# Sorted-block attention with a SwiGLU layer on one core: one weight load cut in two, a smaller mixing matrix, and a new order for the first scores

## The chip, the core and the metric

The kernel runs on one core of a Trainium2 chip. A core has five engines that run side by side, each with its own list of instructions in order: TensorE (PE; its weight loads are shown apart as PEld), VectorE (DVE), ScalarE (ACT), GpSimd (POOL) and SyncE (SP). Sixteen DMA engines move data between DRAM and the core's memory. TensorE writes its results into PSUM, eight banks of 512 float32 values in each of 128 partitions. The metric is the time of one execution in microseconds (us) on the device; less is better.

## The reference

Inputs are q, k and v of shape (4, 8, 768, 64): 4 batches, 8 heads, 768 rows of 64; a matrix sort_net of 8 x 8 for each batch and head; and three weight matrices. Everything is float32.

```python
P = sort_net
for _ in range(5):                       # Sinkhorn: rows, then columns
    P = P - np.max(P, axis=-1, keepdims=True)
    P = np.exp(P)
    P = P / (np.sum(P, axis=-1, keepdims=True) + 1e-09)
    P = P / (np.sum(P, axis=-2, keepdims=True) + 1e-09)
k_sorted = np.einsum('bhij,bhjcd->bhicd', P, k_b)     # 8 blocks of 96 rows are mixed
v_sorted = np.einsum('bhij,bhjcd->bhicd', P, v_b)
scores = scale * np.matmul(q_b, k_sb.transpose(0, 1, 2, 4, 3))   # within each block
attn = softmax(scores)
x = concat_heads(np.matmul(attn, v_sb))               # 3072 tokens x 512
g = x @ w_gate                                        # 512 x 1536
val = x @ w_val
out = (g / (1 + exp(-g)) * val) @ w_out               # 1536 x 512
```

So there is a small normalisation of P, a mixing of key and value blocks by P, attention inside each block of 96 rows, and a SwiGLU layer (FFN) over all 3072 tokens.

## The kernel before, in words

**FFN.** The 3072 tokens are taken as eight token tiles of 384 (`ffn(n)`, n = 0 to 7). In a tile the 1536 hidden columns are taken 128 at a time, m = 0 to 11. `gate(n, m)` (matmuls on L410) and `value(n, m)` (L428) each make four matmuls. ACT takes the tanh (L418), DVE makes the product with the gate (L420) and the product with the value (L433). The output projection of a tile (`outp`, L445) runs during the next tile.

**Attention.** `scores(b, u)` (L332) makes the scores of a unit u of batch b, a unit being 4 blocks of two heads; `exps` takes the exponential on ACT, in one instruction where the two heads sit in one two-bank tile (L345) and in two otherwise (L343). `av` multiplies by the values (L359), and DVE divides by the row sums (reciprocal L363, product `st` L365). The result is transposed (`x_first`, `x_to`, L376) and becomes the FFN's input `xt`.

**Mixing.** Keys, values and queries are brought into the layout that attention wants by matmuls with a block-diagonal matrix `rmix`, in chunks: `q0_chunk` (L274), `k0_chunk` (L284), `v_chunk` (L300) for batch 0, `kq_chunk` (L264) for later batches. A chunk is drained from PSUM by DVE (L242) or ACT (L244), as its argument "v" or "s" says. `vch` holds the values in another layout; POOL (L150) and ACT (L148) copy it from the loaded `v`. `rmix` is made from the Sinkhorn result: DVE writes `p_bf`, the 8 x 8 matrices with eight copies side by side (L236); 16 matmuls (L494) turn this into `w_ps`, 64 rows at a time; `mix_rows` (L499) masks it.

**PSUM tiles** are named by a tag: "a" and "b" hold two banks each, "gen" has three buffers of one bank, "x" is one bank. A new tile in a tag waits until the readers of the one before it have finished.

**The start (L483 to L582)** is written out by hand for TensorE, DVE, ACT and POOL: the order in the source is the order on the engine. Matmuls on zeros (`fill`, and `wide_fill` in float32) stand in places where TensorE has nothing to do. Then `merge` puts attention and mixing of later batches between the FFN's matmuls at written-out times; from there on the planner orders DVE, and TensorE, POOL, ACT and SP keep the source's order.

**Loads.** Nearly all loads are issued by POOL into one queue, with a conversion from float32 to bfloat16 on the way. In order: v of batch 0 (1, 2), q (3), k in two halves (4, 5), then after POOL's three copies into `vch` the weights. `load_gv(lo, hi)` loads the columns lo to hi of the gate weights and then of the value weights (L136): 0 to 255 (loads 6, 7), q again (8), 256 to 511 (9, 10), 512 to 1023 (11, 12), 1024 to 1535 (13, 14), then the first half of v of batch 1 (15). After three mixes on POOL and 16 one-element memsets (`pad`, L509) come k, q and v of batch 1 (16 to 20), the output weights `wo` (21 to 23, L516), and four copies of v of batch 1 into `vch` (L150), which `v_chunk(1, ...)` in `ffn(1)` reads. `kq_chunk(1, ...)` reads k and q of batch 1. SP's queue has the first load of sort_net and later the output stores and transposes.

Of the kernel before, what the change touches and what calls it, by code (L numbers as in the profile page):

```python
# [9 lines left out]
FP32 = mybir.dt.float32  # L10
BF16 = mybir.dt.bfloat16
AF = mybir.ActivationFunctionType
ALU = mybir.AluOpType
# [4 lines left out]
def kernel(  # L18
# [11 lines left out]
    nc = tc.nc  # L30

    B, H, S, D = q.shape
    NB = sort_net.shape[-1]
    C = S // NB
    BH = B * H
# [18 lines left out]
    const = ctx.enter_context(tc.tile_pool(name="const", bufs=1))  # L54
# [83 lines left out]
    def load_gv(lo, hi):  # L138
        load_w(wg_sb, wg_dram, lo, hi)
        load_w(wv_sb, wv_dram, lo, hi)  # L140
# [38 lines left out]
    load_gv(0, 256)  # L179
    load_q0(1)  # L180
    load_gv(256, 512)
    load_gv(512, 1024)
    load_gv(1024, DF)
    load_v(1, 0, 2)

# [6 lines left out]
    def vt_tile(pair):  # L192
        if pair not in vts:
            t = vtp.tile([C, 2, H * NB, D + 8], BF16, name=f"vt{pair}", tag="vt")
            nc.vector.memset(t[:, :, :, D:D + 1].rearrange("p u n e -> p (u n) e"), 1.0)
            vts[pair] = t
        return vts[pair]
# [6 lines left out]

    rowreds = [const.tile([BH, NB, 1], FP32, name=f"rowred{it}") for it in range(N_ITER)]
    colred = const.tile([BH, 1, NB], FP32)
    p_bf = const.tile([BH, NB, 8, NB], BF16)
    w_sb = const.tile([128, NB, B, H], BF16)
    pad = const.tile([1, 16], FP32)
    def pair_tile(name, tag):  # L210
        return psum.tile([128, 1024], FP32, name=name, tag=tag)

# [3 lines left out]
    p_ps = bank_tile("p_ps")[0:BH, 0:NB * NB].rearrange("p (i j) -> p i j", j=NB)  # L216
    for it in range(N_ITER):
        nc.scalar.activation(p_ps, p_sb if it == 0 else p_ps, AF.Exp)
        if it == 1:
            with nc.allow_low_precision("0/1 mask"):  # L220
                nc.vector.tensor_reduce(mask, id4, axis=AX.XY, op=ALU.add)
            nc.scalar.copy(sel, ident.rearrange("p (r g two) -> p two g r", g=H2, two=2))
        if it == 2:
            copy_v(nc.scalar, 0, lowr, 0, cs=slice(24, 34))
            vt_tile(1)
        if it == 3:
            copy_v(nc.scalar, 0, lowr, 0, cs=slice(34, 46))
        rowred = rowreds[it]
        nc.vector.reduce_sum(rowred[:, :, 0], p_ps, axis=AX.X)
        nc.vector.reciprocal(rowred, rowred)  # L230
        nc.vector.tensor_mul(p_ps, p_ps, rowred.to_broadcast([BH, NB, NB]))
        nc.vector.reduce_sum(colred[:, 0, :], p_ps.transpose([0, 2, 1]), axis=AX.X)
        nc.vector.reciprocal(colred, colred)
        if it < N_ITER - 1:
            nc.vector.tensor_mul(p_ps, p_ps, colred.to_broadcast([BH, NB, NB]))
    nc.vector.tensor_tensor(p_bf, p_ps.unsqueeze(2).to_broadcast([BH, NB, 8, NB]),  # L236
                            colred.unsqueeze(1).to_broadcast([BH, NB, 8, NB]), op=ALU.mult)
    copy_v(nc.scalar, 0, lowr, 0, d1=40, cs=slice(46, 72))

    def drain(eng, dst, src):  # L240
# [28 lines left out]
    def q0_chunk(t, at, n, eng, tag):  # L269
        dst = kqt_tile(0)[:, GI * C:2 * GI * C].rearrange("p (g t r c) -> p t g r c", g=H2, t=2, c=QC)[:, t]  # L270
        tp = chunk_tile("tq0", n // 8, tag).rearrange("p (l g r) -> p l g r", l=n, g=H2)
        for lc in range(n):
            for two in range(2):
                nc.tensor.matmul(tp[two * D:(two + 1) * D, lc], lhsT=q0[t][:, at + lc, :],  # L274
                                 rhs=sel[:, two], start=True, stop=True)
        drain(eng, dst[:, :, :, at:at + n], tp.rearrange("p l g r -> p g r l"))

    def k0_chunk(at, n, eng, tag, parts=None):
        dst = kqt_tile(0)[:, 0:GI * C].rearrange("p (n a c) -> p a n c", a=2, c=HC)
        rm = rmix[0].rearrange("p a (g two) i -> p two a g i", two=2)  # L280
        tp = chunk_tile("tk0", n // 8, tag).rearrange("p (l a n) -> p l a n", l=n, a=2)
        for lc in range(n):
            for two in range(2):
                nc.tensor.matmul(tp[two * D:(two + 1) * D, lc].rearrange("p a (g i) -> p a g i", g=H2),  # L284
                                 lhsT=k0[:, at + lc, :], rhs=rm[:, two], start=True, stop=True)
        src = tp.rearrange("p l a n -> p a n l")
        if parts is None:
            drain(eng, dst[:, :, :, at:at + n], src)
            return
        drain(eng, dst[:, :, 0:parts, at:at + n], src[:, :, 0:parts])  # L290
        return lambda e: drain(e, dst[:, :, parts:, at:at + n], src[:, :, parts:])

    def v_chunk(b, at, n, eng, tag):
        rows = slice(0, 128) if b % 2 else lowr
        dst = vt_tile(b // 2)[:, b % 2]
        mix = rmix[b][rows, 0].rearrange("p a b -> p (a b)")
        tp = chunk_tile("tv", n // 8, tag).rearrange("p (l n) -> p l n", n=H * NB)
        for ld in range(n):
            col = (at + ld) * C
            nc.tensor.matmul(tp[:, ld, :], lhsT=vch[rows, col:col + 128], rhs=mix,  # L300
                             start=True, stop=True)
        drain(eng, dst[:, :, at:at + n], tp[0:C].transpose([0, 2, 1]))
# [45 lines left out]
    def qk(b, u, tag="b"):  # L348
        exps(b, u, *scores(b, u, tag))

    def av(b, u, tag="a"):
        half, g = divmod(u, H2)
        vt = vts[b // 2][:, b % 2].rearrange("p (h i) e -> p h i e", h=H)
        av_ps = pair_tile("av_ps", tag).rearrange("p (two n) -> p two n", two=2)
        o = av_ps.rearrange("p two (i e) -> p two i e", i=4)
        for two in range(2):
            e = es[(b, u)][two]
            for i4 in range(4):
                nc.tensor.matmul(o[:, two, i4, 0:D + 1], lhsT=e[:, i4 * C:i4 * C + 128],  # L359
                                 rhs=vt[:, 2 * g + two, half * 4 + i4, 0:D + 1],  # L360
                                 start=True, stop=True)
        r_sb = ssp.tile([C, 2, 4, 1], FP32, name="r_sb", tag="r")
        nc.vector.reciprocal(r_sb, o[0:C, :, :, D:D + 1])  # L363
        st = ssp.tile([C, 4, 2, D], BF16, name="st", tag="st")
        nc.vector.tensor_tensor(st.rearrange("p i two d -> p two i d"), o[0:C, :, :, 0:D],  # L365
                                r_sb.to_broadcast([C, 2, 4, D]), op=ALU.mult)
        sts[(b, u)] = st
# [105 lines left out]
    idle_ps = bank_tile("idle_ps", "x")  # L473

    def fill(tile, n):
        for _ in range(n):
            nc.tensor.matmul(tile, lhsT=warm_sb[:, 0:128], rhs=warm_sb, start=True, stop=True)

    def wide_fill(n):
        for _ in range(n):  # L480
            nc.tensor.matmul(idle_ps, lhsT=wide_sb[:, 0:128], rhs=wide_sb, start=True, stop=True)  # L481

    wide_fill(3)  # L483
    nc.tensor.matmul(idle_ps[0:8, 0:8], lhsT=vch[lowr, 24:32], rhs=vch[lowr, 24:32], start=True, stop=True)
    wide_fill(1)
    fill(idle_ps, 3)
    q0_chunk(0, 0, 8, "s", "x")
    fill(bank_tile("idle_ps"), 2)

    w_ps = bank_tile("w_ps")[:, 0:NB * B * H].rearrange("p (i b h) -> p i b h", b=B, h=H)  # L490

    for i in range(NB):
        for g in range(2):
            nc.tensor.matmul(w_ps[64 * g:64 * g + 64, i].rearrange("p b h -> p (b h)"),  # L494
                             lhsT=p_bf[:, i].rearrange("p a b -> p (a b)"),
                             rhs=ident[0:BH, 0:BH], start=True, stop=True)

# [7 lines left out]
    for b in range(1, B):  # L505
        rows = halves[b % 2]
        mix_rows(nc.gpsimd, rmix["p"][rows, b % 2] if b > 1 else rmix[1][rows, 0], rows, w_sb, b)
    for n in range(16):
        nc.gpsimd.memset(pad[:, n:n + 1], 0.0)  # L509
    for lo, hi in ((0, 2), (2, 4)):  # L510
        load_k(1, lo, hi)
# [12 lines left out]
    k0_chunk(8, 8, "v", "gen")  # L524
    k0_chunk(16, 8, "s", "gen")
    k0_chunk(24, 8, "v", "gen")
    rest = [k0_chunk(32, 8, "s", "x", 2 * NB), k0_chunk(40, 8, "v", "gen", 2 * NB)]
    v_chunk(0, 40, 16, "v", "b")
    v_chunk(0, 56, 8, "s", "gen")
    for drain_rest in rest:  # L530
        drain_rest("v")
    fill(pair_tile("idle_ps", "a")[:, 0:512], 1)
    qk(0, 0, "a")
    qk(0, 1, "b")
    av(0, 0, "a")
    qk(0, 2, "gen")
    idle_ps = bank_tile("idle_ps", "x")
    fill(idle_ps, 1)
    av(0, 1, "b")
    xts[(0, 0)] = xtp.tile([128, H2, TW], BF16, name="xt0_0", tag="xt")  # L540
    qk(0, 3, "mixed")

    def x_first(u, eng, tag):
        x_ps = xt_tile(tag, 1)[:, 0]
# [34 lines left out]
    value_out(0, 1, first[3])  # L579
    q0_chunk(1, 0, 16, "s", "b")  # L580
    q0_chunk(1, 16, 8, "v", "x")
    nc.vector.tensor_copy(rmix[1][lowr, 1].rearrange("p h i -> p (h i)"), ident[lowr, lowr])  # L582
    man.__exit__(None, None, None)
    man = tc.manual_schedule(engines={ET.PE, ET.Pool, ET.Activation, ET.SP})
# [112 lines left out]
```

## Time and profile before

| | |
|---|---|
| Time, median of 3 runs | 244.59 us (244.46 to 245.49) |
| The profiled execution | 243.93 us, its span 242.2 us |
| TensorE busy | 232.7 us (96%) |
| DVE, ACT, POOL busy | 155.6, 112.0, 54.9 us |
| First matmul of the FFN (L559) | at 21.05 us |
| First full gate by `gate` (L410) | at 25.16 us |
| Copies of v of batch 1 into `vch` on POOL | 37.90 to 49.16 us |

All times inside an execution are counted from the start of its span. In a line of the timeline the first number is the start in us, the second the length, then engine, source line, operation, what it writes and reads, their shape and how many instructions were joined; in brackets how long the engine was idle before, and what released it. "Landing" is the moment at which the data of a load is in place; the trace has it for every load.

### The profile page before, as it was taken

How to read it: one execution, taken by the hardware profiler on the slowest of the kernel's cores; microseconds unless marked ns; L12 is line 12 of the kernel's file. 1: busy time of each engine (PE TensorE's matmuls, PEld its weight loads, DVE VectorE, ACT ScalarE, POOL GpSimd, SP SyncE). 2: the span in 40 equal slices, each digit the busy share in tenths (PEclk: the TensorE clock that was granted, in tenths of full speed). 3: DMA queues.
4: the chain of work that ended last, by engine and by line, in shares of the span. 5: the costliest groups of instructions: out<-in, count | busy, mean ns of one | idle time of the engine just before them, and what ended most of it. 6: DMA issues, size and time to landing. Idle time of an engine off the chain costs nothing.

```text
span 242.2 us, 5881 instructions
## 1 busy us (share of the span) xinstructions
PE 232.7 (96%) x2453; PEld 136.8 (56%) x2476; DVE 155.6 (64%) x327; ACT 112.0 (46%) x190; POOL 54.9 (23%) x66
## 2 busy tenths in 40 slices
PE   7789999999999999999999999999999999999994
PEld 3376665775556556555555565565556555555543
DVE  6796889874666585776855765484566477445700
ACT  3977652577526434455454253345325433332212
POOL 5997228970006089000000000000000000000000
PEclk9999999999999999999999999999999999999999
DMA  5989999999936999462122112012111211110122
GB/s 96 214 120 181 206 213 211 206 211 202 174 92 132 186 164 152 90 129 71 37 72 63 35 43 77 3 60 64 35 41 55 67 37 43 43 43 3 43 87 87
DMA packets 40698, 24.76 MB, mean 102 GB/s; under 512 B 29408, under 2 KB 35424, under 8 KB 40672
## 3 DMA queue, kind: packets, MB, share of 16 engines
q0 software_dynamic: 20688, 14.16, 41.2%
q1 hardware_dynamic: 19840, 10.17, 16.7%
q8 instruction: 19, 0.31, 0.5%
q10 hardware_dynamic: 144, 0.07, 0.1%
q14 instruction: 7, 0.06, 0.1%
HBM read 28.32 MB, written 7.86 MB: 149 GB/s over the span
## 4 chain that ended last, share of the span: by engine, by line
PE 85%; DMA 7%; POOL 5%; issue 1%; DVE 1%; ACT 0%; POOLq 0%
PE v_ps L428 25%; PE g_ps L410 25%; PE o_ps L445 24%; DMA wv_sb<-in_moe_w_val_dram 5%; POOL vch L150 3%; PE tkq L264 3%; PE av_ps L359 3%; PE qk L332 2%; DMA v<-in_v_dram 2%; PE tv L310 1%; PE o_ps L461 1%; POOL wg_sb L136 1%; PE tv L300 1%; POOL wv_sb L136 1%; PE x_ps L376 0%
## 5 line engine op out<-in xcount | busy, mean ns | idle before, releaser
L420 DVE SCALAR_TENSOR_TENSOR gs_sb<-th_sb,g_ps 128x384 bf16<-128x384 bf16 x96 | 52.9, 551 | 50.1 <-ACT th_sb L418 47.1
L410 PE MATMUL g_ps<-xt,wg_sb 128*128 128x384 bf16 x376 | 76.6, 325 | 0.1
L428 PE MATMUL v_ps<-xt,wv_sb 128*128 128x384 bf16 x376 | 76.5, 326 | 0.1
L418 ACT ACTIVATE th_sb<-g_ps 128x384 bf16<-128x384 f32 x96 | 47.1, 491 | 57.0 <-PE g_ps L410 54.3
L445 PE MATMUL o_ps<-wo,h 128*128 128x512 bf16 x254 | 61.4, 379 | 1.5 <-issue 0.5
L433 DVE SCALAR_TENSOR_TENSOR h<-v_ps,gs_sb 128x384 bf16<-128x384 f32 x96 | 53.4, 556 | 7.7 <-DVE gs_sb L420 0.5
L428 PEld LDWEIGHTS <-wv_sb 128*128 128x128 bf16 x376 | 35.0, 97 | 23.3 <-issue 0.2
L410 PEld LDWEIGHTS <-wg_sb 128*128 128x128 bf16 x376 | 34.9, 97 | 23.4
L445 PEld LDWEIGHTS <-h 128*128 128x128 bf16 x276 | 26.0, 98 | 28.5
L450 ACT COPY o_sb<-o_ps 128x512 f32<-128x512 f32 x23 | 13.5, 586 | 49.3 <-PE o_ps L445 49.3
L150 POOL COPY vch<-v 64x1536 bf16<-64x1536 bf16 (+2 forms) x11 | 29.4, 2712 | 9.8 <-PE g_ps L410 8.1
L345 ACT ACTIVATE e_all<-qk 96x768 bf16<-96x768 f32 x30 | 23.2, 801 | 3.8 <-PE qk L332 3.7
L365 DVE TENSOR_TENSOR st<-av_ps,r_sb 96x512 bf16<-96x512 f32 x32 | 21.8, 680 | 0.3
L359 PEld LDWEIGHTS <-e_all 96*128 96x128 bf16 x256 | 11.9, 97 | 4.6 <-ACT e_all L345 0.3
L359 PE MATMUL av_ps<-vt,e_all 96*128 96x65 bf16 x256 | 13.0, 193 | 0.2 <-ACT e_all L345 0.2
L244 ACT CAST vt<-tv 96x1024 bf16<-96x1024 f32 (+1 forms) x10 | 9.7, 965 | 4.9 <-PE tv L310 3.5
L363 DVE RECIPROCAL r_sb<-av_ps 96x8 f32<-96x8 f32 x32 | 6.4, 199 | 7.8 <-PE av_ps L359 7.8
L242 DVE CAST vt<-tv 96x1024 bf16<-96x1024 f32 (+1 forms) x8 | 8.0, 1016 | 2.1 <-PE tv L310 1.8
L481 PE MATMUL idle_ps<-wide_sb 128*128 128x512 f32 x8 | 6.4, 954 | 1.5 <-DVE wide_sb L70 1.5
L242 DVE COPY oq_v<-o_ps 128x128 f32<-128x128 f32 x1 | 0.3, 293 | 9.3 <-PE o_ps L461 9.3
L395 POOL DMA_DIRECT2D q_scr<-in_q_dram x2 | 5.6, 2813 | 0.3 <-issue 0.3
L332 PE MATMUL qk<-kqt 64*128 64x96 bf16 x128 | 4.5, 204 | 0.7 <-PE tv L300 0.4
(87 smaller groups left out, 130.8 us busy)
## 6 DMA issues: line engine op xcount, KB each, us to landing
out_dram<-o_sb SPq DMA_DIRECT2D x23, 256.0 KB, 2.0
v<-in_v_dram POOLq DMA_DIRECT2D x4, 384.0 KB, 11.7
wo<-in_moe_w_out_dram POOLq DMA_DIRECT2D x3, 512.0 KB, 16.7
kqp<-in_k_dram POOLq DMA_DIRECT2D x2, 768.0 KB, 10.3
q_scr<-in_q_dram POOLq DMA_DIRECT2D x2, 768.0 KB, 18.4
v<-in_v_dram POOLq DMA_DIRECT2D x2, 768.0 KB, 9.7
wg_sb<-in_moe_w_gate_dram POOLq DMA_DIRECT2D x2, 512.0 KB, 11.9
wv_sb<-in_moe_w_val_dram POOLq DMA_DIRECT2D x2, 512.0 KB, 14.3
```

The source lines that it names most:

```text
L150: eng.tensor_copy(dst, src.transpose([0, 2, 1]))
L244: nc.scalar.copy(dst, src)
L345: nc.scalar.activation(e_all[:, n:n + 2, 0:4 * C], wide[0:C, :, 0:4 * C], AF.Exp, scale=scale)
L359: nc.tensor.matmul(o[:, two, i4, 0:D + 1], lhsT=e[:, i4 * C:i4 * C + 128], rhs=vt[:, 2 * g + two, half * 4 + i4, 0:D + 1], start=True, sto ...
L365: nc.vector.tensor_tensor(st.rearrange("p i two d -> p two i d"), o[0:C, :, :, 0:D], r_sb.to_broadcast([C, 2, 4, D]), op=ALU.mult)
L410: nc.tensor.matmul(g_ps, lhsT=wg_sb[:, kc, ts(m, 128)], rhs=xt[:, kc, :], start=(kc == 0), stop=(kc == NKC - 1))
L418: nc.scalar.activation(th_sb, g_ps, AF.Tanh, scale=0.5)
L420: nc.vector.scalar_tensor_tensor(gs_sb, th_sb, 1.0, g_ps, op0=ALU.add, op1=ALU.mult)
L428: nc.tensor.matmul(v_ps, lhsT=wv_sb[:, kc, ts(m, 128)], rhs=xt[:, kc, :], start=(kc == 0), stop=(kc == NKC - 1))
L433: nc.vector.scalar_tensor_tensor(h_tiles[n][:, m, :], v_ps, 0.5, gs_tiles.pop(m), op0=ALU.mult, op1=ALU.mult)
L445: nc.tensor.matmul(o_ps, lhsT=h_w[:, m, ts(t3, 128)], rhs=wo_sb[part][:, m % 4, :], start=(m == 0), stop=(m == NFC - 1))
L450: nc.scalar.copy(o_sb, o_ps)
```

## The change

Weights 512 to 1023 are loaded as two pairs of 256 columns. The Sinkhorn result is written with four copies instead of eight, and 32 matmuls of 32 rows take the place of 16 of 64. The pad has 14 memsets instead of 16. The memset of the second value tile (`vt_tile(1)`) moves from Sinkhorn round 2 on DVE to the end of the part written by hand. Two fills change. The last 16 rows of keys (32 to 47) go in one chunk into the two-bank tile "a" instead of two chunks in "x" and "gen"; the last values go in three chunks of 8 (56, 40, 48) instead of one of 16 and one of 8; the first scores stand between them. The scores of units 0 to 3 use the tags "b", "gen", "a", "gen" instead of "a", "b", "gen", "mixed", and `av(0, 0)` uses "b" instead of "a".

```diff
-    load_gv(512, 1024)
+    load_gv(512, 768)
+    load_gv(768, 1024)
     load_gv(1024, DF)
     load_v(1, 0, 2)
...
-    p_bf = const.tile([BH, NB, 8, NB], BF16)
+    p_bf = const.tile([BH, NB, 4, NB], BF16)
...
-    pad = const.tile([1, 16], FP32)
+    pad = const.tile([1, 14], FP32)
...
         if it == 2:
             copy_v(nc.scalar, 0, lowr, 0, cs=slice(24, 34))
-            vt_tile(1)
...
-    nc.vector.tensor_tensor(p_bf, p_ps.unsqueeze(2).to_broadcast([BH, NB, 8, NB]),
-                            colred.unsqueeze(1).to_broadcast([BH, NB, 8, NB]), op=ALU.mult)
+    nc.vector.tensor_tensor(p_bf, p_ps.unsqueeze(2).to_broadcast([BH, NB, 4, NB]),
+                            colred.unsqueeze(1).to_broadcast([BH, NB, 4, NB]), op=ALU.mult)
...
-    wide_fill(1)
-    fill(idle_ps, 3)
+    wide_fill(2)
     q0_chunk(0, 0, 8, "s", "x")
...
     for i in range(NB):
-        for g in range(2):
-            nc.tensor.matmul(w_ps[64 * g:64 * g + 64, i].rearrange("p b h -> p (b h)"),
+        for g in range(4):
+            nc.tensor.matmul(w_ps[32 * g:32 * g + 32, i].rearrange("p b h -> p (b h)"),
...
-    for n in range(16):
+    for n in range(14):
         nc.gpsimd.memset(pad[:, n:n + 1], 0.0)
...
-    rest = [k0_chunk(32, 8, "s", "x", 2 * NB), k0_chunk(40, 8, "v", "gen", 2 * NB)]
-    v_chunk(0, 40, 16, "v", "b")
+    drain_rest = k0_chunk(32, 16, "s", "a", 2 * NB)
     v_chunk(0, 56, 8, "s", "gen")
-    for drain_rest in rest:
-        drain_rest("v")
-    fill(pair_tile("idle_ps", "a")[:, 0:512], 1)
-    qk(0, 0, "a")
-    qk(0, 1, "b")
-    av(0, 0, "a")
-    qk(0, 2, "gen")
+    v_chunk(0, 40, 8, "v", "gen")
+    qk(0, 0, "b")
+    v_chunk(0, 48, 8, "v", "x")
+    drain_rest("v")
+    qk(0, 1, "gen")
+    av(0, 0, "b")
+    qk(0, 2, "a")
     idle_ps = bank_tile("idle_ps", "x")
     fill(idle_ps, 1)
     av(0, 1, "b")
     xts[(0, 0)] = xtp.tile([128, H2, TW], BF16, name="xt0_0", tag="xt")
-    qk(0, 3, "mixed")
+    qk(0, 3, "gen")
...
     q0_chunk(1, 16, 8, "v", "x")
+    vt_tile(1)
```

## The prediction, made before the changed kernel was run

> **What bounds the kernel now.** I read the page first, then the chain that ended last, then busy time by stretch, and last the two places where that chain leaves TensorE.
>
> The page: the span, the engines' busy time, and the DMA share in 40 slices of 6.05 us.
>
> ```profile
> span 242.2 us, 5881 instructions
> ...
> PE 232.7 (96%) x2453; PEld 136.8 (56%) x2476; DVE 155.6 (64%) x327; ACT 112.0 (46%) x190; POOL 54.9 (23%) x66
> ...
> DMA  5989999999936999462122112012111211110122
> ```
>
> TensorE (PE) is idle for only 9.5 us. The DMA engines are full from slice 3 to slice 10, about 14.5 to 60 us. The chain that ended last (start, length, what) begins outside TensorE:
>
> ```profile
> 6.26 6.81 POOL vch L150 x3
> ...
> 17.27 12.12 DMA wv_sb<-in_moe_w_val_dram
> 29.44 0.82 PE v_ps L428 x4
> ```
>
> Three GpSimd (POOL) copies, then weight issues, then a landing; from 29.44 us on, nearly all TensorE. By stretch (us, busy PE, PEld, DVE, ACT, POOL, clock, DMA share, GB/s):
>
> ```profile
> 13.84:24.28 10.44, 9.29 (x217) 6.99 (x218) 8.28 (x18) 7.74 (x16) 9.17 (x31) 1.00 1.17 165
> 24.28:49.26 24.98, 24.85 (x369) 16.06 (x369) 22.30 (x47) 13.02 (x22) 15.26 (x11) 1.00 1.17 209
> ```
>
> After 24.28 us TensorE is full at a granted clock of 1.00: 0.13 us idle in 25. So a gain can only come from before 24.28 us, and a gain there survives only if what TensorE needs later is there earlier too. POOL's timeline tells when that is (start, length; idle before, releaser):
>
> ```profile
> 17.27 0.77 POOL L136 DMA_DIRECT2D wv_sb<-in_moe_w_val_dram  x1
> ...
> 19.47 0.65 POOL L102 DMA_DIRECT2D v<-in_v_dram  x1
> ...
> 29.68 0.59 POOL L102 DMA_DIRECT2D kq<-in_q_dram  x1 [2.44 <-DMA wv_sb<-in_moe_w_val_dram]
> ...
> 37.11 0.74 POOL L516 DMA_DIRECT2D wo<-in_moe_w_out_dram  x1 [0.83 <-DMA v<-in_v_dram]
> 37.90 11.26 POOL L150 COPY vch<-v 64x1536 bf16<-64x1536 bf16 x4
> ```
>
> From the 16th POOL load on, load n is issued when load n-8 has landed: the 20th (q of batch 1, 29.68) after the 12th (wv 512 to 1023, landed 29.39), the 23rd (37.11) after the 15th (v of batch 1, landed 36.83). Only then do the four copies of v start; they end at 49.16. TensorE's weight loads (PEld) that use these things:
>
> ```profile
> 46.82 1.09 PEld L264 LDWEIGHTS <-kq 128*64 128x64 bf16 x64 [0.32 <-issue]
> ...
> 49.21 0.56 PEld L300 LDWEIGHTS <-vch 128*128 128x128 bf16 x16 [0.17 <-POOL vch L150]
> ```
>
> The second half of q of batch 1 lands at 29.68 + 17.0 = 46.7 and is read at 46.82: slack 0.15. The last copy ends at 49.16 and is read at 49.21: slack none. Wv 1024 to 1535 lands at 35.26 (18.74 + 16.5) and is read at 36.05: slack 0.79. So TensorE and the load stream reach 49.2 us together, and delaying **either** delays the end.
>
> **The change, part by part.**
>
> *Weights in halves.* Loads 11 and 12 (512 columns) become four of 256. POOL issues two more, at 0.76 us each: its issues after 18.0 us come 1.52 us later. Queued behind them are v of batch 1, three mixes (20.20 to 21.29; read first at 42.3), 14 memsets (two fewer, 0.07 us) and the first k load. All of this is hidden: with load 10 landed at 23.86, seven loads (about 2.4 MB, some 12 us at 204 GB/s) are still queued. The eight places shift by two for both partners, so the last wo load still waits for v of batch 1.
>
> What is not hidden is the size of the packets: 1024 of 1024 bytes become 2048 of 512 bytes, in a queue that is never empty. The rates of this queue at 512 bytes (15 to 17 us) and at 1024 bytes (24 to 31 us), packets, MB, share of 16 engines:
>
> ```profile
> q0 software_dynamic: 740, 0.37, 139.9%
> ...
> q0 software_dynamic: 1439, 1.43, 123.5%
> ```
>
> 0.37 MB in 2 us is 185 GB/s; 1.43 MB in 7 us is 204. The 1.049 MB took 5.13 us and will take 5.67: **+0.54 us** on every later landing. Upper end: packet time, 61.3 ns for 512 bytes and 98.5 for 1024, gives (2048 x 61.3 - 1024 x 98.5)/16 = +1.54. Lower end: landings. The loads of 256 columns numbered 9 and 10 landed 1.06 and 1.41 after the one before, mean 1.235; those of 512 columns (11 to 14) landed 2.85 apart in the mean. 4 x 1.235 - 2 x 2.85 = -0.76. I take +0.54: it is counted in a full queue, while packet times overlap (both shares exceed 100%) and those two landings followed a load of 3072-byte packets.
>
> [...]
>
> The gain of the halves is that value projection 4 (L428 at 29.44) waits for half of wv only. It waited 0.06 us. Gain at most 0.06, and the slacks of 0.15 and 0 behind it take that back.
>
> *Four-fold matrix.* L236: 0.68 us for 512 elements, 0.22 for 64 (L235), so 0.42 for 256: -0.26. The 16 matmuls of L494 took 0.43; 32 take 0.85 at the same 26.7 ns each (+0.42), or 0.43 if four column groups overlap (0). Sum -0.26 to +0.16. Both ends are covered at first: the next stage, k0_chunk, starts at 13.84 because k lands at 13.70, and the v chunks ended 0.15 before. I take +0.1 and let it vanish.
>
> *Memset of vt1, fills.* The 0.17 us leave Sinkhorn round 2, but the exp at 7.56 follows an ACT copy that ends at 7.51: 0. In its new place (about 27 us) DVE has 2.7 us spare up to 49 us: 0, or 0.17 without that. wide_fill(2) for 1 wide and 3 narrow fills ends at 9.4, before the q landing at 9.84: 0.
>
> *Last keys and first scores.* New order, by before's rows. Sixteen keys in "a" end at 15.77; ACT drains the first half (0.59) to 16.41; v56 and v40 follow on PE to 16.24; scores 0 in "b" at 16.46 (was 16.95). ACT drains v56 to 17.0, then exp 0 until 17.75 (was 18.14). DVE: v40 to 16.98, v48 to 17.78, drain_rest (512 elements, 0.69) to 18.38. av(0,0) at 17.85 (was 18.20), reciprocal 18.35, st until 19.27 (was 19.58): 0.31 **gained**. But av(0,1) now also sits in "b", and cannot write before st(0,0) has read it: it starts at 19.33, while before it had its own tile:
>
> ```profile
> 19.05 0.41 PE L359 MATMUL av_ps<-vt,e_all 96*128 96x65 bf16 x8
> ```
>
> 0.28 **lost**. Queued behind av(0,1) on PE are scores 3, the first transpose and av(0,2); DVE idles 0.5 us before the second reciprocal, and nothing in the rest of this stage makes it up. TensorE reaches the FFN at 24.28 + 0.28 = 24.56. Bounds: 0 if the gained 0.31 holds instead, +0.8 if ACT's and DVE's new order costs another drain (0.5).
>
> *Sum.* The two terms do not add: at 49.2 us the later of the two counts. TensorE comes 0.28 late, load stream and copies 0.54. Profiled execution: 243.93 + 0.54 = 244.47 (its span of 242.16 to 242.7, the 1.77 us around it unchanged). That execution lay 0.66 under the median of the runs, so forecast 244.59 + 0.54 = **245.1**.
>
> **Rivals.**
> 1. *The small packets cost their full time* (slower). Place: the q0 queue between 22 and 37 us. Price +1.54, 246.1. For: the per-packet rows. Against: overlap. It decides once v of batch 1 lands after 36.83 + 1.22 = 38.05.
> 2. *The wait for "b" grows* (slower). If drain_rest and the split exp 1 push st(0,0) to 20.2, av(0,1) starts 1.2 late: 245.8. For: DVE is back to back from 16.3. Against: DVE work in this stage is the same.
> 3. *512-byte packets run like 1024-byte ones*: landings unchanged, TensorE's 0.28 left: 244.9. Against: 185 and 204 GB/s. [...]
> 4. *The halves land earlier and TensorE gains* (faster). Landings -0.76; TensorE could win at most its idle time from 13.84 to 20.48, 0.38 + 0.35 + 0.20 + 0.22 = 1.15. Then 243.8. With the 1.06 of load 9 for all four, -1.46, TensorE's 1.15 counts: 243.4. Against: the tile "b".
>
> **How the numbers follow.** 0.5% is 1.22 us, about what a measurement of this kernel can tell from no change. Forecast 0.58, rivals 0.18, 0.08, 0.10 and 0.06. Slower by more: rivals 1 and 2, 0.26. Faster by more: half of rival 4, as only its far end comes near that bound, 0.03. Within: 0.71. The range runs from 244.3 (rival 3 without the 0.28, less 0.3 of scatter) to 246.2 (rival 1 at its full price); beyond it lie about 2 in 10: half of rival 1 (scatter on either side of its price), half of rival 2, and rival 4.
>
> **What the new profile would show.** Right: packets of 512 bytes until about 29 us at 185 GB/s; v of batch 1 landed at 37.4, the four copies from 38.4 to 49.7; a wait on POOL or on q of batch 1 ahead of L264 or L300 at 47 to 50 us, with TensorE back to back afterwards; av(0,0) near 17.85, av(0,1) near 19.33 waiting for st; the FFN's first full gate near 25.4 instead of 25.16. Wrong: that landing at 36.8 or less (rivals 3, 4) or past 38 (rival 1); the FFN's start past 25.5 (rival 2); or new idle time of TensorE after 50 us, which no step here expects.

## The result

The changed kernel takes 246.45 us (median of 17 runs, 244.81 to 247.21), the kernel before 244.77 us (17 runs in turn with it, 244.05 to 245.74). The ratio is 1.0055, its 95% interval 1.0034 to 1.0076: slower, by about the 0.5% that was named as the bound. The forecast was 245.1.

The 17 times fall into three groups, and what parts them is a number that the prediction had read once and then left alone: the granted clock of TensorE.

| Mean granted clock of the run | Runs | Mean time |
|---|---|---|
| 1.000 | 3 | 245.21 us |
| 0.993 | 6 | 245.92 us |
| 0.983 to 0.986 | 8 | 246.98 us |

At full clock the kernel is where the forecast put it. In 14 of 17 runs the mean granted clock was 0.993 or less. The profiled execution (246.85 us, clock 0.984) is of the third group; it shows where. Two runs of the experiments below (248.11 us of the kernel before, 248.39 us of one version) lie over 1.5% above the fastest run of their kernel and are left out of the ratios, though not of the medians and counts.

### The profile page after: what moved, and what is told of

Its sections match the earlier page's. It is cut to its first block, busy times and chain, and to the rows that moved or that the text cites. A ratio compares the mean times of both kernels' runs of the same rounds, so it can differ in the third digit from the quotient of the medians.

```text
span 245.1 us, 5910 instructions
## 1 busy us (share of the span) xinstructions
PE 234.7 (96%) x2468; PEld 138.2 (56%) x2490; DVE 155.2 (63%) x326; ACT 112.3 (46%) x190; POOL 56.2 (23%) x66
## 4 chain that ended last, share of the span: by engine, by line
PE 89%; DMA 4%; DVE 3%; issue 1%; POOL 1%; ACT 0%; DVEq 0%; POOLq 0%
PE v_ps L428 25%; PE g_ps L410 24%; PE o_ps L445 24%; DMA qk<-in_k_dram 4%; PE av_ps L359 3%; PE tkq L264 3%; PE qk L332 3%; PE tv L310 1%; PE o_ps L461 1%; PE tv L300 1%; PE g_ps L557 1%; PE x_ps L376 1%; PE v_ps L557 1%; PE tk L284 1%; DVE h L433 1%
## 5 line engine op out<-in xcount | busy, mean ns | idle before, releaser
L420 DVE SCALAR_TENSOR_TENSOR gs_sb<-th_sb,g_ps 128x384 bf16<-128x384 bf16 x96 | 53.1, 553 | 50.8 <-ACT th_sb L418 47.8
L359 PEld LDWEIGHTS <-e_all 96*128 96x128 bf16 x256 | 12.6, 101 | 5.3 <-ACT e_all L345 0.6
L359 PE MATMUL av_ps<-vt,e_all 96*128 96x65 bf16 x256 | 13.7, 198 | 0.7 <-DVE vt L242 0.6
L242 DVE CAST vt<-tv 96x512 bf16<-96x512 f32 (+1 forms) x9 | 8.1, 921 | 2.5 <-PE tv L310 1.8
```

What stands on the lines that cost most here:

```text
L420: nc.vector.scalar_tensor_tensor(gs_sb, th_sb, 1.0, g_ps, op0=ALU.add, op1=ALU.mult)
```

## The profile after

From the page, the lines that answer to those of before, and the row of the clock:

```profile
span 245.1 us, 5910 instructions
...
PE 234.7 (96%) x2468; PEld 138.2 (56%) x2490; DVE 155.2 (63%) x326; ACT 112.3 (46%) x190; POOL 56.2 (23%) x66
...
PEclk9995999999999999999999999999999999999999
DMA  5989999999925999734121212012111211110122
```

The fourth slice (18.4 to 24.5 us) has a 5 where all the others have a 9. The stretches (us, busy PE, PEld, DVE, ACT, POOL, granted clock, DMA share, GB/s), cut at the edges of that fall:

```profile
15.43:18.84 3.41, 2.45 (x64) 2.02 (x63) 2.69 (x6) 2.60 (x6) 3.41 (x6) 1.00 1.31 170
18.84:25.67 6.83, 6.71 (x59) 4.33 (x59) 3.33 (x8) 2.96 (x6) 4.44 (x22) 0.50 1.35 191
25.67:49.26 23.59, 22.96 (x301) 14.60 (x300) 20.17 (x45) 11.95 (x21) 16.02 (x12) 1.00 1.19 209
```

From 18.84 to 25.67 us, 6.83 us or twice 3.41, TensorE ran at half clock. It was busy for 6.71 us of it, so nearly everything in there took longer. Its timeline:

```profile
17.85 0.40 PE L359 MATMUL av_ps<-vt,e_all 96*128 96x65 bf16 x8 [0.55 <-DVE vt L242]
18.45 0.34 PE L332 MATMUL qk<-kqt 64*128 64x96 bf16 x8 [0.20 <-DVE kqt L242]
...
19.38 0.60 PE L359 MATMUL av_ps<-vt,e_all 96*128 96x65 bf16 x8
...
22.16 0.52 PE L557 MATMUL v_ps<-xt,wv_sb 128*128 128x384 bf16 x1
...
27.63 0.82 PE L410 MATMUL g_ps<-xt,wg_sb 128*128 128x384 bf16 x4
```

av(0,0) took 0.40 us; av(0,1), the same eight matmuls, took 0.60 after the edge. An FFN matmul follows the one before by 0.32 us instead of 0.16. The first full gate comes at 27.63 us, 2.47 later than before; the span ends 2.9 later. The load stream does not set this end: POOL's copies of v of batch 1 end at 49.45 us, and TensorE reads them only from here on:

```profile
52.04 0.67 PEld L300 LDWEIGHTS <-vch 128*128 128x128 bf16 x16
```

The runs of before show the fall too, but rarely: in the three comparisons below, 9 of its 103 runs had a clock of 0.993 or less.

## The experiments

Three theories were tried against each other. **Clock:** TensorE has too little to do between about 15 and 19 us, and the clock is halved for one or two periods of 3.41 us. **Load:** smaller packets delay the loads of batch 1. **Tile:** av(0,1) waits for the tile "b". All kernels were timed in 12 runs (one in 11), beside 34 or 35 of the kernel before. "Low" is a run with a mean clock of 0.993 or less; "full clock" is any other.

| Kernel | Median us | Ratio to before (95%) | Low runs | Mean at full clock |
|---|---|---|---|---|
| before, in the three comparisons | 244.98, 244.81, 244.76 | | 4 of 35, 4 of 34, 1 of 34 | 244.95, 244.86, 244.89 |
| changed, three fills | 245.08 | 1.0009 (0.9991 to 1.0026) | 1 of 12 | 245.05 |
| changed, wide weights | 245.77 | 1.0032 (1.0005 to 1.0058) | 9 of 12 | 244.72 |
| before, halved weights | 244.73 | 0.9987 (0.9966 to 1.0009) | 0 of 12 | 244.83 |
| before, two fills less | 245.32 | 1.0017 (0.9997 to 1.0037) | 11 of 12 | 244.25 (1 run) |
| before, one fill less | 244.80 | 1.0006 (0.9984 to 1.0027) | 4 of 12 | 244.79 |
| changed, dropped fill restored | 246.85 | 1.0071 (1.0049 to 1.0093) | 10 of 11 | 246.33 (1 run) |
| changed, three fills, av tiles in turn | 244.93 | 1.0010 (0.9986 to 1.0033) | 1 of 12 | 245.08 |
| changed, three fills, memset back | 245.28 | 1.0017 (0.9994 to 1.0040) | 2 of 12 | 245.26 |
| before, new order only | 245.25 | 1.0024 (1.0003 to 1.0045) | 10 of 12 | 244.70 (2 runs) |
| changed, old order | 245.39 | 1.0027 (0.9998 to 1.0056) | 5 of 12 | 245.01 |
| changed, two fills ahead of av(0,0) | 245.14 | 1.0013 (0.9994 to 1.0033) | 1 of 12 | 245.17 |
| changed, three fills, tiles in turn, memset back | 244.96 | 1.0009 (0.9989 to 1.0029) | 1 of 12 | 245.07 |

**Three fills in the changed kernel.** Matmuls on zeros where TensorE was idle.

```diff
     v_chunk(0, 40, 8, "v", "gen")
+    fill(pair_tile("idle_ps", "b")[:, 0:512], 1)
     qk(0, 0, "b")
...
     qk(0, 1, "gen")
+    fill(bank_tile("idle_ps"), 2)
     av(0, 0, "b")
```

> The changed kernel with three matmuls on zeros more: one in "b" ahead of the first scores, two in a "gen" tile ahead of av(0,0), all in places where TensorE was idle (16.4 and 17.3 to 17.85 us). Clock theory (the granted clock is halved for one or two periods of 3.4 us from about 19 us because TensorE does too little between 15 and 19 us): clock 1.00 in nearly all runs, time near that of the changed kernel's runs at clock 1.00, 245.0 to 245.4, ratio to before 1.001 to 1.003. Load theory (the smaller packets alone make the difference) or tile theory (the wait for "b" alone): the fills change nothing, 246.4, ratio 1.0055, clock again 0.984 to 0.993 in most runs.

Low runs fell from 14 of 17 to 1 of 12, and the ratio from 1.0055 to 1.0009. The added work makes the kernel faster: it stands in idle time, and the clock stays up (a mean of 0.998 or more in 11 of 12 runs). Its stretch and timeline:

```profile
18.84:25.67 6.83, 6.35 (x116) 4.21 (x115) 4.13 (x10) 4.16 (x9) 3.50 (x7) 1.00 1.31 180
```

```profile
17.23 0.61 PE L477 MATMUL idle_ps<-warm_sb 128*128 128x512 bf16 x2
17.90 0.40 PE L359 MATMUL av_ps<-vt,e_all 96*128 96x65 bf16 x8
...
19.43 0.40 PE L359 MATMUL av_ps<-vt,e_all 96*128 96x65 bf16 x8 [0.26 <-DVE st L365]
...
25.54 0.82 PE L410 MATMUL g_ps<-xt,wg_sb 128*128 128x384 bf16 x4
...
28.74 0.81 PE L428 MATMUL v_ps<-xt,wv_sb 128*128 128x384 bf16 x4 [0.50 <-DVE gs_sb L420]
```

The same stretch has clock 1.00. As nothing is stretched here, other effects can be read too: the wait for "b" (0.26 us ahead of av(0,1)), the first full gate at 25.54, and a new wait of 0.50 us at 28.74. The clock theory held; load and tile, which had promised no change, did not.

**Fills taken out of the kernel before.** First two, the one that the change drops and the one after the third scores:

```diff
-    fill(pair_tile("idle_ps", "a")[:, 0:512], 1)
     qk(0, 0, "a")
...
-    idle_ps = bank_tile("idle_ps", "x")
-    fill(idle_ps, 1)
     av(0, 1, "b")
```

> The kernel before without the two matmuls on zeros between the last values and av(0,1) (the one ahead of the first scores, which the change drops, and the one after the third scores). Clock theory: TensorE's activity between 16 and 19.5 us falls by 0.43 us of 3.4, the clock falls to half from about 19 us in a good part of the runs, those 0.7 to 1.8 us longer; median 0.3 to 1.5 us above before. Load and tile theories: nothing changes, ratio 0.999 to 1.001.

The mean clock was 0.993 or less in 11 of 12 runs, where the kernel before had 4 of 35. No other work was touched. In time this costs little: the median rises by 0.34 us, and the interval of the ratio (0.9997 to 1.0037) reaches below 1. The stretches of its profile, cut at the fall:

```profile
16.87:20.29 3.42, 2.26 (x54) 1.66 (x51) 3.19 (x7) 3.26 (x7) 3.35 (x6) 1.00 1.15 177
20.29:23.70 3.41, 3.21 (x25) 2.19 (x26) 1.84 (x5) 1.69 (x4) 2.60 (x21) 0.50 1.34 185
```

One period at half clock follows a period in which TensorE was busy for 2.26 us of 3.42. Then only the first of the two, the one that the change drops:

```diff
-    fill(pair_tile("idle_ps", "a")[:, 0:512], 1)
     qk(0, 0, "a")
```

> The kernel before without the one matmul on zeros that the change drops (into "a", ahead of the first scores); the other stays. Clock theory: with both dropped 11 of 12 runs showed a clock of 0.993 or less; with one, TensorE loses 0.21 us of work in a period of 3.4 us instead of 0.43, so fewer, 2 to 8 of 12, median 0 to 0.4 us above before. If the new order of the change and not the dropped fill lowers the clock: 0 to 1 of 12, ratio 1.000.

4 of 12, and the time as before: by itself the dropped fill costs no time that shows. Its matmul is easily overlooked, for no trace of a kernel that has it holds a record of it, only of its weight load. In the kernel before:

```profile
16.50 0.10 PEld L477 LDWEIGHTS <-warm_sb 128*128 128x128 bf16 x1
...
16.95 0.35 PE L332 MATMUL qk<-kqt 64*128 64x96 bf16 x8 [0.38 <-PE tv L300]
```

Without that fill the first scores start at 16.36 us in this kernel's profile. So the 0.38 us that look idle hold work, and a busy share of TensorE that takes in this place is too low where the fill stands.

**Which idle time it is.** The changed kernel with only the dropped fill restored (into "b", ahead of the first scores):

```diff
     v_chunk(0, 40, 8, "v", "gen")
+    fill(pair_tile("idle_ps", "b")[:, 0:512], 1)
     qk(0, 0, "b")
```

> The changed kernel with one matmul on zeros restored (into "b", ahead of the first scores). Clock theory with the dropped fill as its cause: low clock in at most 3 of 12 runs (14 of 17 in the changed kernel), time 245.0 to 245.4. If the new order, with its idle 0.55 us ahead of av(0,0), takes part: 4 to 9 of 12, 245.4 to 246.2.

10 of 11 low, and 246.85 us: more than either expectation gave. Why it takes longer than the changed kernel (246.45) was not tried. The idle time ahead of av(0,0) is still there in its profile:

```profile
18.06 0.40 PE L359 MATMUL av_ps<-vt,e_all 96*128 96x65 bf16 x8 [0.61 <-DVE vt L242]
```

And with only the two fills ahead of av(0,0):

```diff
     qk(0, 1, "gen")
+    fill(bank_tile("idle_ps"), 2)
     av(0, 0, "b")
```

> The changed kernel with only the two matmuls on zeros ahead of av(0,0), where TensorE idles 0.55 us; the dropped one is not restored. With the dropped one alone restored the clock was low in 10 of 11 runs. If the idle time ahead of av(0,0) is what counts: low clock in at most 4 of 12 runs, 245.0 to 245.5. If all three are needed: 7 or more of 12, 245.6 or more.

1 of 12. Two fills in the idle 0.55 us ahead of av(0,0) are enough, and the dropped fill is not what was missing. As two matmuls were added here and one there, the place and the amount of the added work are not told apart. TensorE idles there because it waits for DVE to drain the last values, which the new order puts into two drains of 512 elements, the second of them behind the first scores.

**Which part of the change it is.** The new order alone, in the kernel before:

```diff
-    rest = [k0_chunk(32, 8, "s", "x", 2 * NB), k0_chunk(40, 8, "v", "gen", 2 * NB)]
-    v_chunk(0, 40, 16, "v", "b")
+    drain_rest = k0_chunk(32, 16, "s", "a", 2 * NB)
     v_chunk(0, 56, 8, "s", "gen")
...
-    fill(pair_tile("idle_ps", "a")[:, 0:512], 1)
...
+    v_chunk(0, 40, 8, "v", "gen")
+    qk(0, 0, "b")
+    v_chunk(0, 48, 8, "v", "x")
+    drain_rest("v")
...
```

> The kernel before with the new order of the last keys, last values and first scores only (the dropped matmul on zeros included); loads, four-fold matrix, pad, memset and the fills at 7.6 us as before. If the order alone lowers the clock: low clock (0.993 or less) in 9 or more of 12 runs, median 245.6 to 246.8, and no wait of 0.5 us near 29 us. If it needs the other parts: low clock in 4 or fewer, 244.8 to 245.2.

10 of 12 low, nine of them with one period only by their mean clock of 0.993, and no wait of 0.5 us near 29 us. The median, 245.25, stays below the 245.6 to 246.8 expected. In its profile the same 0.55 us stand ahead of av(0,0):

```profile
17.80 0.40 PE L359 MATMUL av_ps<-vt,e_all 96*128 96x65 bf16 x8 [0.55 <-DVE vt L242]
```

The rest of the change with the old order:

```diff
-    drain_rest = k0_chunk(32, 16, "s", "a", 2 * NB)
+    rest = [k0_chunk(32, 8, "s", "x", 2 * NB), k0_chunk(40, 8, "v", "gen", 2 * NB)]
+    v_chunk(0, 40, 16, "v", "b")
     v_chunk(0, 56, 8, "s", "gen")
...
```

> The changed kernel with the old order of keys, values and first scores and its matmul on zeros; loads in halves, four-fold matrix, pad, memset's new place and fills as changed. If the order is the cause: low clock in at most 3 of 12 runs, 244.8 to 245.3, with the wait of about 0.5 us near 29 us still there (memset). If the other parts lower the clock: 9 or more of 12, 246 or more.

5 of 12, between the two expectations; the wait near 29 us is 0.22 us, not the 0.5 expected. Its profile has a fall in another place:

```profile
10.58:13.99 3.41, 2.42 (x105) 2.07 (x104) 2.78 (x7) 3.03 (x4) 3.41 (x4) 1.00 0.63 126
13.99:17.40 3.41, 3.35 (x109) 3.32 (x110) 2.08 (x4) 1.64 (x4) 3.41 (x6) 0.50 1.13 144
```

In the period ahead of it TensorE waits for k to land:

```profile
14.04 2.77 PE L284 MATMUL tk<-rmix,qk 128*64 128x64 bf16 x96 [0.76 <-DMA qk<-in_k_dram]
```

In the other eight profiles with the changed start this wait is 0.30 to 0.50 us. So the order lowers the clock in more runs (10 of 12 against 5 of 12), but by time the two parts of the change cannot be told apart (1.0024 and 1.0027), and the order alone does not make up the 1.0055. The changed start (fills, four-fold matrix, earlier end of the value chunks) can lead to a fall too, though with the new order and the fills ahead of av(0,0) only 6 of 60 runs were low. Which of its parts does so was not tried.

**The load in halves.** The changed kernel with one pair of 512 columns (and 16 memsets in the pad):

```diff
-    load_gv(512, 768)
-    load_gv(768, 1024)
+    load_gv(512, 1024)
```

> The changed kernel with columns 512 to 1023 loaded as one pair again (and 16 pad memsets). Clock theory: the clock still falls in most runs, median 245.9 to 246.5, ratio 1.004 to 1.007. Load theory: v of batch 1 lands 0.3 to 0.5 earlier than in the changed kernel, ratio back to 1.000 to 1.002.

Low in 9 of 12: the clock falls without the halves too. The ratio of 1.0032 lies between the two expectations; three runs of the 12 kept the clock, and six lost one period only by their mean clock of 0.993. The kernel before with halves alone (the same lines the other way, 14 memsets):

> The kernel before with columns 512 to 1023 loaded as two pairs (and 14 pad memsets), nothing else. Load theory by the counted rates: v of batch 1 lands at 37.1 to 37.4 instead of 36.8, the copies of v and the end are 0.3 to 0.54 later, ratio 1.0012 to 1.0022. By packet times +1.54: ratio 1.006. Clock theory: clock as in the kernel before.

No loss shows: 0.9987, and the upper end of the interval, 1.0009, is +0.22 us, less than half of the +0.54 forecast. v of batch 1 landed at 36.80 us, in the kernel before at 36.83. POOL's wait and the first copy in this profile, beside 37.11 and 37.90 before:

```profile
37.09 0.74 POOL L517 DMA_DIRECT2D wo<-in_moe_w_out_dram  x1 [0.94 <-DMA v<-in_v_dram]
37.87 2.85 POOL L150 COPY vch<-v 64x1536 bf16<-64x1536 bf16 x1
```

One profile settles little, for that landing scatters: 36.30 to 38.82 in the five profiles with wide weights (mean 37.2), 36.55 to 39.22 in the nine with halves (mean 37.6).

**Tiles in turn.** av(0,1) in "a", so that it need not wait for st(0,0), on top of the three fills; the next users of "a" and "b" (the first value projection of the second column, the q chunk) are swapped with them:

```diff
-    qk(0, 2, "a")
+    qk(0, 2, "gen")
...
-    av(0, 1, "b")
+    av(0, 1, "a")
...
-    av(0, 2, "a")
+    av(0, 2, "b")
...
-    av(0, 3, "b")
+    av(0, 3, "a")
```

> The changed kernel with the three fills, and with av(0,1) in "a", av(0,2) in "b", av(0,3) in "a", the third scores in "gen" (the following users of "a" and "b" swapped). Tile theory: av(0,1) starts at about 19.1 instead of 19.4 and the first full gate at 25.2 instead of 25.5; clock at 1.00. For the end, if it is set by TensorE alone: 0.3 less than with the fills alone, 244.75; if by the loads: no less, 245.05.

av(0,1) starts 1.10 us after av(0,0) instead of 1.53 (19.30 after 18.20, 19.43 after 17.90), so the wait is real and goes away. But av(0,0) itself is later in this profile, and the first full gate comes at 25.48 us instead of the 25.2 expected. The time does not move (245.08 and 245.05 at full clock).

**The memset back in Sinkhorn round 2**, on top of the three fills:

```diff
             copy_v(nc.scalar, 0, lowr, 0, cs=slice(24, 34))
+            vt_tile(1)
...
     q0_chunk(1, 16, 8, "v", "x")
-    vt_tile(1)
```

> The changed kernel with the three fills, and the memset of the second value tile back in Sinkhorn round 2. In the changed kernel and with the fills TensorE waits 0.50 us for the product on L420 ahead of a value projection near 28.7 us. If the memset's new place is the cause, that wait falls to 0.2 or less, and the time by 0.2 to 0.5 to 244.6 to 244.85; if not, wait and time stay (245.05).

The wait of 0.50 us is gone: the value projection follows the scores at once.

```profile
27.83 0.51 PE L333 MATMUL qk<-kqt 64*128 64x96 bf16 x16
28.27 0.82 PE L429 MATMUL v_ps<-xt,wv_sb 128*128 128x384 bf16 x4
```

The time did not fall (245.26 at full clock, where 244.6 to 244.85 was expected), and the profile shows one way in which a gain is lost. TensorE's weight loads:

```profile
50.98 0.52 PEld L301 LDWEIGHTS <-vch 128*128 128x128 bf16 x16 [1.47 <-POOL vch L150]
```

v of batch 1 landed at 38.61 us in this execution, POOL's copies ended late, and TensorE waited for them.

**All of it**: three fills, tiles in turn, memset back, by the three diffs above.

> The changed kernel with the three fills, the first av tiles in turns (av(0,1) in "a"), and the memset back in Sinkhorn round 2: clock 1.00, no wait of 0.5 us near 29 us, first full gate at 25.2 to 25.5. If the loads of batch 1 set the end, its time is that of the kernel before, 244.6 to 245.0, and a wait on POOL or q of batch 1 shows at 47 to 51 us; if TensorE alone sets it, 0.3 to 0.5 less than with the fills and the tiles alone (245.08 at full clock), 244.6 or less, and less than before.

244.96, ratio 1.0009: no version here is shown to beat the kernel before. The first full gate comes at 25.91 us in its profile, later than expected. TensorE again waits for POOL, as the expectation's load branch had it:

```profile
50.12 0.52 PEld L301 LDWEIGHTS <-vch 128*128 128x128 bf16 x16 [0.56 <-POOL vch L150]
```

## Why the prediction was right or wrong

The forecast was no change by the bound, at 245.1; the result is 246.45 and a ratio just over the bound. The range (244.3 to 246.2) ends below that median; the ratio applied to the before of the prediction, 244.59 x 1.0055 = 245.9, lies in it. That is luck: the range reached up to 246.2 for the sake of small packets, which cost little or nothing, and no part of it was drawn for the clock. The rise by the ratio is 1.35 us where 0.54 was forecast.

*What bounds the kernel.* Wrong in one sentence: "TensorE is full at a granted clock of 1.00". The clock was read as a property of the stage, and the fills show that it depends on what TensorE has to do (14 of 17 runs low without the three fills, 1 of 12 with them). This is the step that failed, and no rival named it. The 17 runs give the size: mean 246.29, against 245.21 in the three at full clock, so 1.08 us are the clock's, more than the rest together. Nor did the load stream set the end, as the forecast of +0.54 has it: in the changed kernel's profile the copies of v were done 2.6 us before TensorE read them (49.45 and 52.04).

*Fills.* "wide_fill(2) for 1 wide and 3 narrow fills ... 0", and the fill dropped ahead of the first scores was not costed at all. Their time is indeed hidden; their effect on the clock was not seen. Rival 4 even counts the 0.38 us ahead of the first scores as idle time, where this fill stood. Taking two fills out of the kernel before brought the clock down in 11 of 12 runs.

*The order of keys and scores.* Right in its times: av(0,0) forecast and measured at 17.85, av(0,1) at 19.33 against 19.38 in the changed kernel (by then at half clock) and 19.43 with fills, the first full gate at 25.44 (24.56 plus 0.88) against 25.54 with fills. What the step missed is that the order leaves 0.55 us idle ahead of av(0,0), which its own numbers held: scores 0 from 16.46, sixteen short matmuls behind them, and av(0,0) only at 17.85.

*Weights in halves.* The mechanism (smaller packets in a full queue) was mis-sized. The rate for 512 bytes was taken from 15 to 17 us, right after the queue had been almost still (0 and 23 GB/s between 13.4 and 14.8 us). The queue's rows for 24 to 27 us (packets, MB, share), before and changed:

```profile
q0 software_dynamic: 616, 0.61, 123.5%
```

```profile
q0 software_dynamic: 1186, 0.59, 145.2%
```

0.59 against 0.61 MB in 3 us: 197 and 203 GB/s, so 1.049 MB cost about 0.17 us more, not 0.54. Of the 9% between 185 and 204 GB/s that the forecast took, 3% remain. Rival 1 (+1.54) is excluded by the run with the halves alone (at most +0.22). In the changed kernel v of batch 1 landed at 37.10 us, where 37.4 was forecast and the kernel before has 36.83; the scatter between executions is too large to tell these apart. Also missed: with two loads more, the sixteenth is wv 1024 to 1535 and waits for the eighth, q of batch 0, which landed at 22.01:

```profile
22.30 0.74 POOL L136 DMA_DIRECT2D wv_sb<-in_moe_w_val_dram  x1 [2.15 <-DMA qk<-in_q_dram]
```

It delayed POOL's mixes to 23.72, which was hidden as claimed.

*Four-fold matrix.* Right: L236 took 0.41 us (forecast 0.42). The 32 matmuls took 0.37 us in all, where the 16 of before took 0.42; so the lower end (0) held, not the 0.85 us of the upper one, nor the value taken (+0.1); k landed at 13.58 and covered it either way.

*Memset.* Costed at 0, "or 0.17 without that"; it cost a wait of 0.50 us on TensorE, which went away when the memset was put back. DVE's spare time over 25 us did not help, because the memset runs beside a product for which TensorE is waiting: with it that product (L420) ends 1.02 us after the drain before it, without it 0.54. With the old order TensorE's wait there is only 0.22 us, so the price is not the memset's alone.

*Sum.* That a delay at 25 us and a late landing do not add up fits the two waits of TensorE for POOL's copies near 50 us (1.47 and 0.56 us). At full clock the changed kernel is at 245.21 (3 runs) and 244.9 before: +0.3 beside the forecast of +0.54, a size that came near the forecast for partly other reasons.

## What to carry to other kernels

A matmul on zeros in idle time can be what keeps the clock up (14 of 17 runs low in the changed kernel, 1 of 12 with two such matmuls ahead of av(0,0)). Before one is dropped, or work is reordered so that TensorE waits in a stage of small matmuls, see how much of a period (3.41 us here) TensorE is busy. That share is a hint and no proof (72% was followed by a fall in the changed kernel and by none in the version with the two fills), so look at the granted clock of many runs, not of one profile. Read rates from a stretch in which the queue has been full for some time (for 512 bytes 185 GB/s right after a pause here, 197 later). And where two streams arrive together, as TensorE and POOL's copies do here near 49 us, an edit to one of them alone may gain nothing.

## What the runs showed of the hardware

In six of the 14 profiles the granted clock fell to 0.50. In the changed kernel it stayed there for 6.83 us, two periods of 3.41; in the five others for one: 20.29 to 23.70 us with two fills less, 20.64 to 24.05 with the dropped fill restored, 19.76 to 23.18 with the new order alone, 13.99 to 17.40 with the old order, and with the wide weights about 21 to 24.5, where the matmuls of the FFN follow each other by 0.30 to 0.33 us (mean clock 0.993).

In the changed kernel the clock falls once more at 244.13 us, after the last matmul: 218.45 us, or 64 times 3.413, after its rise at 25.67. In the kernel before that is the only fall, at 241.98. So the edges of this one execution lie on a grid of 3.413 us, and the grid lies otherwise in the other: counted back, it begins 5.19 us after the start in the changed kernel and 6.46 in the kernel before. That fits the runs of one kernel with no, one and two low periods: 3.41 us at 0.50 take 0.007 from the mean clock of a span of 245 us, and the means are 1.000, 0.993 and 0.983 to 0.986.

In five of the six profiles the stretches show the period just ahead of the fall: TensorE was busy for 66 to 72% of it (2.26 of 3.42, 2.45 of 3.41, 2.42 of 3.41 are shown above; 2.34 of 3.41 with the dropped fill restored, 2.35 of 3.41 with the new order alone). The share alone does not decide it, though. With the two fills ahead of av(0,0), a period of 72% (2.47 of 3.41, from 15.36 us) was followed by one at 1.00. So were the period from 5.19 us in the changed kernel, with 61% (2.10 of 3.42), and that from 6.46 us in the kernel before, with 64% (2.18 of 3.41). And the first low period was 96% busy in the changed kernel (3.29 of 3.41), where a second followed, and 94 to 100% in four others (3.21, 3.20 and 3.35 of 3.41, 3.42 of 3.42), where none did. For comparison, the kernel before in its profile:

```profile
16.70:20.11 3.41, 2.60 (x61) 2.10 (x61) 2.95 (x7) 3.18 (x6) 3.41 (x5) 1.00 1.15 173
```

76%, and somewhat more with the fill that has no record; the clock stayed at 1.00 behind it. No period here was idle: the falls followed periods with 28 to 34% of idle time among small matmuls. Whether it is the time busy or the amount of arithmetic that counts was not tried.

What makes the landing of v of batch 1 scatter by 2.5 us between executions stays open.
